# One kernel, two orders of issue: another table of ranks for the same instructions

## The chip, the core and the metric

The kernel runs on one core of one Trainium2 chip. A core has five engines, each with its own stream of instructions that it issues in order: TensorE (PE in the profile, with its weight load PEld), VectorE (DVE), ScalarE (ACT), GpSimd (POOL) and SyncE (SP), which here issues all transfers. The metric is the time of one execution on the device in microseconds, as the median of several runs.

## The reference

`x` is 2048 tokens by 576 channels. The output is the sum of three things: `x`, a spectral filter of the normalised `x`, and a mixture of very small experts on the normalised `x`.

```python
x = A_x
xn = _layernorm(x, axis=-1)
return x + _A_ref(xn, ...) + _B_ref(xn, ...)

# _A_ref: filter in the frequency domain
X = rfft2(x, axes=(-2, -1))
y = irfft2(X * (w_r + 1j * w_i), (S, D))

# _B_ref: 32 heads, two key tables of 8, one expert of 64 for each head and token
q = einsum("nd,dhc->nhc", xf, w_q);  q1, q2 = q[..., :128], q[..., 128:]
i1 = argmax(q1 @ k1.T);  i2 = argmax(q2 @ k2.T)     # K = 1
e = i1 * 8 + i2                                     # the softmax over one candidate is 1
out = sum over heads of gelu(xf . u[e]) * v[e]
```

## The kernel before

**Spectral half.** The two-dimensional transform is split into steps that are matrix products with constant tables. `ln(t, n)` and `folds(t)` normalise a tile of 128 rows and add and subtract its mirrored halves. `dft128(t)`, for 16 tiles, is the first step along the tokens; its results are kept as f16 high and low parts in `AB` and `ABL`. Then come 16 groups `g`. `d_fwd(g)` transforms along the channels, `s_fwd(g)` does the second step along the tokens for two groups at once (it is called for even `g` and makes one pair), `s_mul(g)` multiplies with the spectral weights, `s_inv(g)` and `d_inv(t)` go back. In `s_mul(g)` VectorE makes two products per group (`t1`, `t2`; four per pair), reading PSUM; POOL combines them to `y`; ACT rounds to f16 (`yh`); POOL computes the low part; ACT copies a slice of it to `yl`. `s_inv(g)` needs `yh` and `yl`, and it writes `AB` and `ABL` again by way of ACT and VectorE. The weights of a pair, `Wt`, have three buffers (`Wt_0_110`, `Wt_1_111`, `Wt_2_112`), the tables `s16` four; `load_w(g)` and `load_s16(g)` issue their transfers on SP.

**Expert half.** The keys are folded into the query weights: `fold_part(b, s)` multiplies slices `w` of `w_q` (32 transfers of 576 KB into five buffers) with `KP`, `turned` and `parted` transpose and scale the result into `MU` and `MUL`, 128 rows of heads and keys. `x_t(t)` makes transposed f16 high and low parts of the normalised tile (ACT, POOL `hl`, a transposing transfer on SP). Per block `r` of two tiles, `scores(r)` is one product of `MU` and these, `route(r)` finds the maximum and its index on VectorE (`mx`, `w`, `MT`), and `combine(r)` builds the coefficients of the 64 experts, transposed by TensorE. `fin(t, y)` adds the last step of the inverse transform, the experts' output and `x`, and sends the tile out.

**Order.** The code of these functions doesn't run as it is written. Each call is recorded as an operation of a plan, with its dependencies. Every PSUM tile has one of seven kinds, and at most `LIMIT` tiles of a kind are in flight:

```python
LIMIT = {"x": 2, "a": 4, "b": 4, "c": 4, "s": 2, "f": 1, "m": 2}
```

`a` is `d_fwd` and `d_inv`, `b` is `s_fwd`, `c` is `s_inv`; a tile takes one or two of the eight banks. `forward` then builds the streams: whenever an engine of its model is free, it takes, of the operations whose inputs are there, the one with the smallest number in the table `RANK` (one number for each of 1272 operations). The streams are then issued in that order (line 526, so every instruction has this line in the profile):

```python
_, order, slot, start = self.forward([-r for r in RANK])
...
for i in order:
    for fn, args, kw in ops[i].calls:
        fn(*[x.place() if isinstance(x, _Ps) else x for x in args], ...
```

The same call gives each PSUM tile its place among the banks. On the chip an engine then works through its stream in order and waits at each instruction for what that instruction needs.

Of the kernel before, what the change touches and what calls it, by code (L numbers as in the profile page):

```python
# [32 lines left out]
def _consts():  # L33
# [102 lines left out]
CHANGE = 97.0  # L136

RANK = (
# [63 lines left out]
)  # L202
LIMIT = {"x": 2, "a": 4, "b": 4, "c": 4, "s": 2, "f": 1, "m": 2}
# [1014 lines left out]
```

## Time and profile before

| | us |
|---|---|
| median of 3 runs | 223.99 (223.98 to 224.19) |
| the profiled execution | 224.18 |
| its span in the trace | 222.4 |
| busy: PE | 197.0 (89%) |
| busy: DVE | 190.0 (85%) |
| busy: POOL | 139.8 (63%) |
| busy: ACT | 133.9 (60%) |
| transfers | 48.15 MB, 38.33 read from HBM and 4.72 written there |

The span is what the trace shows from the first to the last event; 1.8 us of the profiled execution lie outside it. Rows of the trace name the tile that is written, an arrow, and the tiles read, with buffer numbers left out: `banks<-s,yh` is a matmul of `s_inv`, `t<-banks,wx,Wt` a product of `s_mul`, `banks<-A,s` is `s_fwd`, `banks<-c,AB` and `banks<-c,ABL` are `d_fwd` or `d_inv`, `banks<-w,KP` is the fold, `banks<-MU,xT` is `scores`. "[0.62 <-DVE t L526]" behind a row says that the engine was idle for 0.62 us ahead of it, and which work ended last that it had waited for.

### The profile page before, as it was taken

How to read it: one execution, taken by the hardware profiler on the slowest of the kernel's cores; microseconds unless marked ns; L12 is line 12 of the kernel's file. 1: busy time of each engine (PE TensorE's matmuls, PEld its weight loads, DVE VectorE, ACT ScalarE, POOL GpSimd, SP SyncE). 2: the span in 40 equal slices, each digit the busy share in tenths (PEclk: the TensorE clock that was granted, in tenths of full speed). 3: DMA queues.
4: the chain of work that ended last, by engine and by line, in shares of the span. 5: the costliest groups of instructions: out<-in, count | busy, mean ns of one | idle time of the engine just before them, and what ended most of it. 6: DMA issues, size and time to landing. Idle time of an engine off the chain costs nothing.

```text
span 222.4 us, 5915 instructions
## 1 busy us (share of the span) xinstructions
PE 197.0 (89%) x2274; PEld 133.6 (60%) x2274; DVE 190.0 (85%) x411; ACT 133.9 (60%) x281; POOL 139.8 (63%) x198
## 2 busy tenths in 40 slices
PE   0289598999998998889999699999999999999993
PEld 0246446785766666675745564654576565678872
DVE  1999999997579978675899989999999998997553
ACT  2279869799938887996686795646541231233320
POOL 2978986860358543794445868769566274657890
PEclk9999979999999999999999999999999999999999
DMA  7999999999999999766170621403452350278935
GB/s 169 378 426 422 406 409 403 392 338 331 302 313 406 288 316 302 193 138 180 42 197 16 160 58 35 111 0 72 92 130 87 106 162 0 60 217 263 409 119 212
DMA packets 33388, 48.15 MB, mean 217 GB/s; under 512 B 20688, under 2 KB 23504, under 8 KB 32976
## 3 DMA queue, kind: packets, MB, share of 16 engines
q1 hardware_dynamic: 33360, 47.77, 66.4%
q8 instruction: 18, 0.29, 0.5%
q14 instruction: 10, 0.08, 0.1%
HBM read 38.33 MB, written 4.72 MB: 194 GB/s over the span
## 4 chain that ended last, share of the span: by engine, by line
PE 56%; DVE 22%; DMA 8%; ACT 5%; issue 4%; POOL 2%; SPq 1%; POOLq 0%; DVEq 0%
PE banks L526 56%; DMA w<-in_wq_dram 7%; DVE t L526 6%; DVE w L526 5%; DVE MT L526 4%; DVE A L526 2%; DMA XN<-in_x_dram 2%; DVE mx L526 1%; DVE AB L526 1%; POOL yh L526 1%; ACT AB L526 1%; DVE sc L526 1%; DVE ABL L526 1%; ACT t L526 1%; ACT yl L526 1%
## 5 line engine op out<-in xcount | busy, mean ns | idle before, releaser
L526 PE MATMUL banks<-MU,xT 128*128 128x512 f16 x192 | 46.8, 379 | 0.7 <-DVE t L526 0.4
L526 POOL TENSOR_TENSOR hl<-XN,hl 128x576 f16<-128x576 f32 x16 | 21.2, 1325 | 24.8 <-ACT hl L526 24.4
L526 PE MATMUL banks<-c,AB 128*128 128x145 f16 (+1 forms) x384 | 35.3, 227 | 0.0
L526 PEld LDWEIGHTS <-xT 128*128 128x128 f16 x224 | 19.7, 98 | 24.1 <-issue 5.5
L526 PEld LDWEIGHTS <-AB 128*128 128x128 f16 x384 | 32.4, 122 | 2.8 <-issue 1.3
L526 POOL TENSOR_TENSOR t<-XN 128x289 f32<-128x289 f32 x32 | 25.3, 809 | 9.3 <-DMA XN<-in_x_dram 3.8
L526 POOL TENSOR_TENSOR A<-t 128x145 f32<-128x145 f32 (+2 forms) x48 | 28.6, 612 | 2.2 <-DVE t L526 0.7
L526 POOL TENSOR_TENSOR y<-t,t 128x289 f32<-128x289 f32 x32 | 22.3, 714 | 10.9 <-DVE t L526 10.5
L526 ACT ACTIVATE yh<-banks,sc 128x580 f32<-128x580 f32 x16 | 11.8, 744 | 24.3 <-PE banks L526 19.3
L526 DVE SCALAR_TENSOR_TENSOR t<-banks,wx,Wt 128x578 f32<-128x578 f32 x32 | 24.5, 808 | 2.0 <-PE banks L526 1.3
L526 POOL TENSOR_TENSOR yh<-y,yh 128x578 f16<-128x578 f32 x16 | 20.7, 1302 | 7.5 <-ACT yh L526 4.2
L526 DVE TENSOR_TENSOR AB<-banks,AB 128x512 f16<-128x512 f32 x32 | 21.7, 680 | 3.9 <-ACT ABL L526 3.3
L526 PE MATMUL banks<-w,KP 128*32 128x288 f32 x256 | 22.4, 449 | 2.5 <-DMA w<-in_wq_dram 1.5
L526 ACT ACTIVATE AB<-banks 128x512 f16<-128x512 f32 x32 | 19.0, 595 | 8.7 <-PE banks L526 8.7
L526 PE MATMUL banks<-Rs,yl 128*99 128x128 f32 x64 | 12.0, 317 | 12.5 <-ACT Rs L526 10.6
L526 PE MATMUL banks<-A,c 128*128 128x288 f32 x64 | 21.7, 421 | 0.5 <-ACT MT L526 0.5
L526 PE MATMUL banks<-c,ABL 99*128 99x289 f16 (+1 forms) x64 | 18.6, 291 | 1.3 <-DVE t L526 0.6
L526 PEld LDWEIGHTS banks<-Rs,yl 128*99 128x99 f32 x64 | 8.7, 186 | 16.8 <-ACT Rs L526 12.6
L526 PEld LDWEIGHTS banks<-Rs,A 128*128 128x128 f32 x128 | 16.4, 203 | 3.2 <-DVE A L526 1.4
L526 DVE TENSOR_REDUCE MT<-w 128x128 bf16<-128x896 bf16 (+1 forms) x16 | 18.2, 1142 | 0.1
L526 PE MATMUL banks<-Rs,A 128*128 128x128 f32 x128 | 18.0, 290 | 0.0
L526 POOL TENSOR_TENSOR t<-yh 128x288 f32<-128x288 f32 x16 | 11.2, 702 | 10.7 <-ACT yh L526 10.6
(106 smaller groups left out, 418.6 us busy)
## 6 DMA issues: line engine op xcount, KB each, us to landing
w<-in_wq_dram SPq DMA_DIRECT2D x32, 576.0 KB, 7.3
Wt<-in_W_dram SPq DMA_DIRECT2D x8, 578.0 KB, 4.3
w<-in_x_dram SPq DMA_DIRECT2D x8, 576.0 KB, 4.6
out_dram<-w SPq DMA_DIRECT2D x14, 288.0 KB, 3.8
XN<-in_x_dram SPq DMA_DIRECT2D x3, 1282.0 KB, 13.4
s<-in_s_dram SPq DMA_DIRECT2D x16, 192.0 KB, 3.1
XN<-in_x_dram SPq DMA_DIRECT2D x2, 641.0 KB, 5.3
c<-in_c_dram SPq DMA_DIRECT2D x1, 868.5 KB, 8.3
```

The costliest lines, as they stand in the source:

```text
L526: fn(*[x.place() if isinstance(x, _Ps) else x for x in args], **{k: x.place() if isinstance(x, _Ps) else x for k, x in kw.items()})
```

## The change

The table `RANK` holds other numbers. Nothing else differs: the same operations with the same dependencies, on the same engines, with the same buffers. By the order in which they come the PSUM tiles get places in the same way as before.

```diff
 RANK = (
-    2, 11, 10, 12, 49, 94, 8, 9, 5, 6, 3, 4, 1, 34, 38, 35, 39, 7, 0, 15, 17, 20, 13, 18, 21, 24, 23, 26, 28,
...
+    33, 36, 55, 25, 37, 40, 56, 57, 45, 63, 14, 16, 19, 28, 22, 42, 31, 98, 66, 107, 111, 97, 101, 44, 39, 50,
...
```

What moves is seen in the streams. Three places follow.

On TensorE, the second pair of spectral groups, before: the end of `s_inv(3)` (tiles `s16_3`, `yl_1`), then two pieces of the fold (`w`, `KP`), the transposes of the folded weights (`c32`, `MT`) and a third piece of the fold, all ahead of `s_inv(2)` (`s16_2`, `yh_0`).

```order
L526 MATMUL banks_66<-s16_3_116,yl_1_104 99x128
L526 MATMUL banks_66<-w_0_117,KP_73 32x288 x4
L526 MATMUL banks_66<-w_3_120,KP_73 32x288 x4
L526 MATMUL banks_66<-c32_68,MT_79 128x128 x3
L526 MATMUL banks_66<-c32_68,wm_81 1x128
L526 MATMUL banks_66<-w_2_119,KP_73 32x288 x4
L526 MATMUL banks_66<-c32_68,MT_79 128x128 x3
L526 MATMUL banks_66<-c32_68,mxr_83 128x1
L526 MATMUL banks_66<-c32_68,MT_79 128x128 x3
L526 LDWEIGHTS yh_0_132
L526 MATMUL banks_66<-s16_2_115,yh_0_132 128x128
```

And after, at the start of `s_inv(2)`, with the end of `d_fwd(7)` (`AB`) ahead of it:

```order
L526 LDWEIGHTS AB_74
L526 MATMUL banks_66<-c16_72,AB_74 128x145
L526 LDWEIGHTS AB_74
L526 MATMUL banks_66<-c16_72,AB_74 128x145
L526 MATMUL banks_66<-w_1_118,KP_73 32x288 x4
L526 MATMUL banks_66<-c32_68,wm_81 1x128
L526 LDWEIGHTS yh_0_132
L526 MATMUL banks_66<-s16_2_115,yh_0_132 128x128
```

`s_inv(2)` has moved ahead of the transposes and of these pieces of the fold, and stands ahead of `s_inv(3)`, behind `d_fwd(6)` and `d_fwd(7)` with one piece of the fold between.

On VectorE, before: the routing of the first block (`mx_0`, `w_2`, `MT`) up to its last sum, then the products of `s_mul(10)` and `s_mul(11)` (`t1`, `t2` with `Wt_0`).

```order
L526 TENSOR_TENSOR w_2_119<-w_2_119,wt_107 128x896
L526 TENSOR_REDUCE MT_79<-w_2_119 128x128
L526 TENSOR_SCALAR wx_82<-banks_66 128x2
L526 RECIPROCAL wx_82<-wx_82 128x2
L526 SCALAR_TENSOR_TENSOR MT_79<-mx_0_127,MT_79 128x128
L526 TENSOR_TENSOR w_2_119<-MT_79,iv_108 128x512
L526 SCALAR_TENSOR_TENSOR MT_79<-MT_79 128x64
L526 TENSOR_TENSOR w_2_119<-w_2_119,MT_79 128x512 x2
L526 TENSOR_REDUCE MT_79<-w_2_119 128x32
L526 SCALAR_TENSOR_TENSOR t1_1_96<-banks_66,wx_82,Wt_0_110 128x578
L526 SCALAR_TENSOR_TENSOR t2_0_105<-banks_66,wx_82,Wt_0_110 128x578
L526 SCALAR_TENSOR_TENSOR t1_0_95<-banks_66,wx_82,Wt_0_110 128x578
```

And after:

```order
L526 SCALAR_TENSOR_TENSOR t1_0_95<-banks_66,wx_82,Wt_0_110 128x578
L526 SCALAR_TENSOR_TENSOR t2_0_105<-banks_66,wx_82,Wt_0_110 128x578
L526 SCALAR_TENSOR_TENSOR t2_1_106<-banks_66,wx_82,Wt_0_110 128x578
L526 TENSOR_TENSOR ABL_75<-banks_66,ABL_75 33x2x128
L526 TENSOR_TENSOR AB_74<-banks_66,AB_74 128x4x128
L526 SCALAR_TENSOR_TENSOR t1_1_96<-banks_66,wx_82,Wt_0_110 128x578
L526 TENSOR_TENSOR AB_74<-banks_66,AB_74 128x4x128
L526 TENSOR_TENSOR ABL_75<-banks_66,ABL_75 33x2x128
L526 TENSOR_REDUCE mx_0_127<-banks_66 128x128
L526 TENSOR_REDUCE mxr_83<-banks_66 1x1
L526 TENSOR_TENSOR w_2_119<-banks_66,mx_0_127 128x896
L526 TENSOR_TENSOR A2_2_99<-banks_66,A2_2_99 128x578
```

The four products of this pair now stand ahead of the first block's maximum `mx_0`, and the routing begins behind them.

On SP, before: the transfers around the weights for `s_mul(4)` and on (`Wt`), with the slices of `w_q` (`w`), the tables `s16` and a transposing transfer between them.

```order
L526 DMA w_2_119<-in_wq_dram 128x1152
L526 DMA Wt_0_110<-in_W_dram 128x1156
L526 DMA w_1_118<-in_wq_dram 128x1152
L526 DMA w_0_117<-in_wq_dram 128x1152
L526 DMA w_3_120<-in_wq_dram 128x1152
L526 DMA s16_1_114<-in_s16_dram 128x768
L526 DMA_TRANSPOSE xT_1_88<-hl_0_122 128x9x128
L526 DMA Wt_1_111<-in_W_dram 128x1156
L526 DMA s16_0_113<-in_s16_dram 128x768
L526 DMA Wt_2_112<-in_W_dram 128x1156
L526 DMA s16_3_116<-in_s16_dram 128x768
L526 DMA w_4_121<-in_wq_dram 128x1152
```

And after, where the same weights are asked for:

```order
L526 DMA w_1_118<-in_wq_dram 128x1152
L526 DMA s16_2_115<-in_s16_dram 128x768
L526 DMA w_0_117<-in_wq_dram 128x1152
L526 DMA Wt_2_112<-in_W_dram 128x1156
L526 DMA s16_3_116<-in_s16_dram 128x768
L526 DMA w_2_119<-in_wq_dram 128x1152
L526 DMA w_3_120<-in_wq_dram 128x1152
L526 DMA Wt_0_110<-in_W_dram 128x1156
L526 DMA w_4_121<-in_wq_dram 128x1152
L526 DMA w_0_117<-in_wq_dram 128x1152
L526 DMA w_1_118<-in_wq_dram 128x1152
```

Here `Wt_2` and the second load of `Wt_0` (the weights of pairs 8 and 10) stand ahead of the last slices of `w_q`; before, `Wt_0` for pair 10 came behind all of them.

Other moves: ahead of the first `d_fwd` the last three tiles of `dft128` change places, and two pieces of the fold (`fold_part(2,0)`) go from just ahead of `d_fwd(0)` to ten operations behind it. The fold as a whole and the transposes to `MU` end later on TensorE; `scores(0)` starts ten operations later; the inverse steps `s_inv` end earlier. At the end the last four output groups are the same, and the transposes of `combine(7)` stand five output groups ahead of the end, where eleven us of work followed them before.

122 rows, old and new, of the table RANK are left out of this document.

## The prediction

> **What bounds the kernel now.** I read the busy time by stretches of the span first, since it shows stage by stage which engine is full. The columns are the stretch, its length, the busy time of TensorE (PE), of the weight load, of VectorE (DVE), ScalarE (ACT) and GpSimd (POOL), then TensorE's granted clock, the DMA share and the rate.
>
> ```profile
> core 0: us, PE busy (x) PEld busy (x) DVE busy (x) ACT busy (x) POOL busy (x), PEclk, DMA share, GB/s
> 0.00:10.00 10.00, 0.28 (x1) 0.29 (x2) 5.19 (x21) 2.64 (x5) 5.47 (x17) 1.00 0.84 259
> 10.00:30.00 20.00, 16.39 (x120) 10.85 (x119) 19.39 (x58) 16.17 (x47) 17.17 (x32) 0.93 1.01 416
> 30.00:50.00 20.00, 18.54 (x171) 14.24 (x164) 18.72 (x45) 16.30 (x45) 14.52 (x23) 0.98 1.01 383
> 50.00:60.00 10.00, 10.00 (x127) 6.87 (x129) 6.52 (x16) 9.95 (x18) 1.28 (x1) 1.00 0.96 311
> 60.00:80.00 20.00, 18.96 (x347) 13.06 (x347) 17.45 (x38) 14.06 (x29) 12.85 (x14) 1.00 1.06 332
> 80.00:100.00 20.00, 17.45 (x319) 13.10 (x318) 15.64 (x37) 17.87 (x35) 12.82 (x15) 1.00 0.85 232
> 100.00:120.00 20.00, 19.59 (x277) 12.01 (x276) 15.95 (x29) 14.88 (x25) 9.85 (x12) 1.00 0.47 121
> 120.00:140.00 20.00, 17.85 (x245) 10.71 (x239) 19.27 (x37) 14.14 (x28) 14.84 (x16) 1.00 0.28 71
> 140.00:200.00 60.00, 58.88 (x546) 37.59 (x545) 58.98 (x118) 22.69 (x47) 36.54 (x53) 1.00 0.37 96
> 200.00:222.40 22.40, 19.01 (x154) 14.93 (x152) 12.88 (x23) 5.21 (x9) 14.47 (x22) 0.99 0.70 250
> sum 222.40, PE 196.97 PEld 133.63 DVE 190.00 ACT 133.91 POOL 139.81; mean PE 19.70 PEld 13.36 DVE 19.00 ACT 13.39 POOL 13.98
> ```
>
> TensorE works 196.97 us and is idle for 25.4. Taken row by row, the idle time is 9.7 us before the first matmul, 5.1 in 10 to 50 (where VectorE is the full engine, 38.1 of 40), 3.6 in 50 to 100, 2.6 in 100 to 140, 1.1 in 140 to 200 and 3.4 in the last row. A change of order can only win from 5.1 + 3.6 + 2.6 + 1.1 = 12.4 us; the rest is the start and the end. From 120 on VectorE is full too (78.25 of 80 us up to 200), so there a wait that is taken from TensorE returns unless VectorE also got ahead.
>
> Then the waits of TensorE, in total and one by one (start, duration, what was idle before and what released it):
>
> ```profile
> PE banks L526 <- DVE t L526: 3.4, 7, 1.0
> ```
>
> ```profile
> 71.09 0.85 PE L526 MATMUL banks<-s,yh 64*128 64x128 f16 x24 [0.62 <-DVE t L526]
> ...
> 85.28 0.30 PE L526 MATMUL banks<-c,ABL 99*128 99x289 f16 x1 [0.40 <-DVE ABL L526]
> ...
> 89.80 0.27 PE L526 MATMUL banks<-c,wm 128*1 128x128 f32 x1 [0.78 <-ACT t L526]
> ...
> 96.67 0.85 PE L526 MATMUL banks<-s,yh 64*128 64x128 f16 x24 [0.54 <-DVE t L526]
> ...
> 123.27 0.85 PE L526 MATMUL banks<-s,yh 64*128 64x128 f16 x24 [1.01 <-DVE t L526]
> ...
> 125.92 0.28 PE L526 MATMUL banks<-c,ABL 99*128 99x289 f16 x1 [0.34 <-DVE t L526]
> ```
>
> The largest single releaser after the start is `DVE t`, the multiplication with the spectral weights in `s_mul`, which frees the PSUM banks of `s_fwd`. `s_inv` cannot be written into them earlier.
>
> **The change, term by term.** No instruction is added or removed, so TensorE's 196.97 us stay. What counts is how much of the 12.4 us of idle time the new order fills.
>
> *Broken runs.* Equal matmuls in a row are cheaper than apart:
>
> ```profile
> 58.20 0.69 PE L526 MATMUL banks<-w,KP 128*32 128x288 f32 x8
> ...
> 63.46 1.18 PE L526 MATMUL banks<-w,KP 128*32 128x288 f32 x16
> ```
>
> Two such groups apart cost 2 × 0.69 − 1.18 = 0.20 us more by busy time; by the starts of the instructions behind them (58.20 to 58.82, 63.46 to 64.57) it is 2 × 0.62 − 1.11 = 0.13. The order has 23 runs of the fold where there were 24, and 158 runs of like groups in all where there were 172. I take −0.1, with ends −0.4 (a few of the other joins worth the same) and 0.
>
> *The start, to 55 us.* TensorE has the same work ahead of the first `d_fwd` (40.3 us by the durations of before). The last three tiles of the first transform change places, and 1.1 us of the fold, the row above of 16 calls, goes from ahead of `d_fwd(0)` to ten places behind it; the loads of weights swap places on SP's queue with the transfers at a share of 1.0. VectorE is the bound, with 1.9 us idle of 40. It cannot gain more than that. I take +0.2, since the fold that leaves was a cover for TensorE while VectorE finished the last tile, and ends −0.5 and +1.1 (the whole fold left uncovered).
>
> *50 to 100 us, waits of 3.6 now.* Pair (2,3) becomes tighter: between the end of `s_fwd(2)` and the first `s_inv` of that pair TensorE has 6.4 us of other work (7.0 before), 7.7 us to the second (12.4 before), by summed durations of the instructions that the order puts there. What the operands need is in these rows, of PE, DVE, POOL and ACT:
>
> ```profile
> 66.73 2.00 PE L526 MATMUL banks<-A,s 64*64 64x289 f16 x48
> ...
> 69.50 2.27 DVE L526 SCALAR_TENSOR_TENSOR t<-banks,wx,Wt 128x578 f32<-128x578 f32 x3
> ...
> 74.22 0.80 DVE L526 SCALAR_TENSOR_TENSOR t<-banks,wx,Wt 128x578 f32<-128x578 f32 x1
> ...
> 66.84 2.53 POOL L526 TENSOR_TENSOR yh<-y,yh 128x578 f16<-128x578 f32 x2
> 69.32 1.21 POOL L526 TENSOR_TENSOR hl<-XN,hl 128x576 f16<-128x576 f32 x1
> 71.19 1.34 POOL L526 TENSOR_TENSOR y<-t,t 128x289 f32<-128x289 f32 x2 [0.66 <-DVE t L526]
> ...
> 75.42 0.52 ACT L526 ACTIVATE yl<-yh 128x396 f16<-128x396 f16 x1
> ...
> 80.81 0.52 ACT L526 ACTIVATE yl<-yh 128x396 f16<-128x396 f16 x1
> ```
>
> `s_fwd(2)` ended at 68.73, the operands were complete at 75.94 and 81.33: 7.2 and 12.6 us later. The second was late because one of its four multiplications stood back on VectorE until 74.22. The new order puts all four together (4 × 0.76 = 3.0 us by the row of three). Then POOL has its y at 3.0 + 1.34 = 4.4, its hl at 5.6, the two low parts at 6.9 and 8.2, and ACT adds 0.52 each: ready at 7.4 and 8.7, against 6.4 and 7.7 of cover. That is a wait of 1.0 in all in place of 0.62. On the other side `d_fwd(8)` now has `s_inv(3)` and two folds more between itself and `s_inv(2)`, whose copies it waited 0.40 for, and pair (4,5) has 8.9 and 12.0 us of cover (7.0 and 9.8 before), so the 0.54 at 96.67 goes. The 0.78 for ACT I halve: ACT is at 17.87 of 20 there, and its work isn't less. Against these stands a new wait. `MU`, the folded weights, is complete only just ahead of its first use:
>
> ```profile
> 95.86 0.27 PE L526 MATMUL banks<-c,xT 128*128 128x128 f32 x1
> ...
> 99.93 0.31 DVE L526 SCALAR_TENSOR_TENSOR MUL<-banks,sc,MUL 128x112 f16<-128x112 f32 x1
> ```
>
> From that last transpose to the last row of `MUL` it took 4.1 us; the new order leaves 1.4 us of TensorE's work between. VectorE does it behind the four multiplications of `s_mul(8)` and `s_mul(9)`. The ends are 2.7 us (as before) and 0 (transpose, copy and scaling at once); I take 0.7, as the copies themselves are short and TensorE is by then not ahead of VectorE by much. Sum: 1.0 + 0.4 + 0.7 and 0.7 for small waits as now = 2.8, so −0.8. The ends are −2.5 (only the 1.0 stays) and +4 (the rival below).
>
> *100 to 140 us, waits of 2.6 now.* `s_inv(9)` waited 1.01 at 123.27 for rows that VectorE had not reached, since the whole of `route(0)` stood ahead of them:
>
> ```profile
> 112.34 1.09 DVE L526 TENSOR_REDUCE mx<-banks 128x128 f32<-128x896 f32 x1 [0.18 <-PE banks L526]
> ...
> 119.82 1.22 DVE L526 TENSOR_REDUCE MT<-w 128x32 f32<-128x1024 bf16 x1
> 120.95 2.26 DVE L526 SCALAR_TENSOR_TENSOR t<-banks,wx,Wt 128x578 f32<-128x578 f32 x3
> ```
>
> That is 8.6 us of routing ahead of `s_mul(10)`; now it stands behind `s_mul(10)` and `s_mul(11)`. Work ahead of `s_mul(10)` on VectorE falls from 101 to 92 us, and on `s_mul(12)` from 114 to 102. The 1.01 and the 0.34 go. What is queued behind is the routing: `scores(0)`'s maximum stands behind 5 us more of VectorE's work, `scores(0)`'s matmuls behind 5.9 us more of TensorE's, so the banks of `scores` come free about when they did against the work around them. I take −1.0; ends −2.0 (0.6 left) and +1.5 (the two largest waits again, for banks of `scores` now).
>
> *After 140 us.* Waits of 1.1 on TensorE, VectorE full. The spectral inverses are done earlier, the routing of the first blocks later, and the sums are equal: 0, ends −0.8 and +1.0.
>
> *The end.*
>
> ```profile
> 207.39 0.28 PE L526 MATMUL banks<-id,MT 128*128 128x128 f16 x2
> ...
> 218.60 0.41 PE L526 MATMUL banks<-vS,MT 128*128 128x288 f16 x2
> ...
> 219.05 0.52 DVE L526 SCALAR_TENSOR_TENSOR w<-banks,sc,w 128x288 f32<-128x288 f32 x1 [0.21 <-PE banks L526]
> ```
>
> The last four output groups are the same. The transposes of `combine(7)` move to 3.7 us ahead of TensorE's end (five groups of 0.73, against 11 us before); VectorE's work ahead of `combine(7)` is unchanged, and its transposes ran at 207.39; 3.7 us ahead of the end is about 214, so they find their input there. 0.
>
> *SP's queue.* The weight loads of `s_mul(4)` to `s_mul(10)` now stand ahead of the last slices for the fold, and SP waits in order for the buffer of each. By the same walk the last three slices are issued when `s_mul(5)` is done, about 84 us, and used from 91 on; with the DMA share at 0.85 in that row they fit. 0.
>
> Sum: −0.1 + 0.2 − 0.8 − 1.0 = −1.7 against the profiled execution's 224.18 us, that is 222.5; the median of the runs, 223.99, lies 0.2 below it. Forecast 222.3.
>
> **Rivals.** *Slower: the pairs need as long as they did.* If POOL and ACT get to the low parts of pair (2,3) no sooner than in before, TensorE waits 0.8 for the first and then 12.6 − 7.7 − 0.8 = 4.1 us for the second, 4.9 in place of the 1.0 that I took: the 2.8 becomes 6.7, and the sum +2.2, that is 226.2. For it speaks ACT at 9.95 of 10 in 50 to 60. Against it speaks that VectorE held back one multiplication, and the new order doesn't. It decides if the second operand comes later than 10.4 us after `s_fwd(2)`, where the added wait eats the 1.7.
>
> *No change: the waits only move.* VectorE is full from 120 on; if TensorE arrives 1.7 us earlier and finds the banks of the routing taken, the time returns by 200. 224.0. Against it: VectorE has 4.4 + 4.1 us idle in 80 to 120 to get ahead in.
>
> *The shared port.* One row of routing shows VectorE held up by POOL:
>
> ```profile
> 114.03 1.28 POOL L526 TENSOR_TENSOR yh<-y,yh 128x578 f16<-128x578 f32 x1 [1.10 <-issue]
> ...
> 114.67 1.12 DVE L526 TENSOR_TENSOR w<-w,wt 128x896 bf16<-128x896 bf16 x1
> ...
> L526 DVE TENSOR_TENSOR w<-w,wt x8: 610/612/1123, 114.7 to 190.2; 128x896 bf16<-128x896 bf16 x8
> ```
>
> It took 1.12 us where the median of eight is 0.61, having begun while POOL's yh ran (to 115.31). The move puts POOL's y and yh of `s_mul(10)` and `s_mul(11)` beside `route(0)`, that is beside four more such operations. At 0.51 us for each, three hits give 1.5 us on a full engine, and the time is 223.8. The other seven of these eight lay clear of it, so I take none.
> The Trainium skill (SBUF — State Buffer, who interferes with whom) says that a VectorE operation with both inputs in SBUF and a GpSimd operation lock each other out for a whole instruction. The rows above agree; by the rule alone all four could be held, and the sum would be 2.0 us worse.
>
> *A larger gain.* If the 0.7 for `MU` and the small waits don't come and VectorE stays ahead, the terms go to −3.3: 220.7.
>
> **Chances.** Near the forecast (221.2 to 223.4) 0.48, larger gain 0.13, waits only moved 0.10 and the port 0.05 (both about 224), slower 0.24. A difference of 0.2% (0.45 us) is about what a measurement tells from none. Faster by more 0.62, within 0.14, slower by more 0.24. The range reaches from the larger gain to the slower case, 220.6 to 225.9; the likeliest case's own is 221.2 to 223.4.
>
> **What would show it.** In the trace after: the wait of `s_inv` on `DVE t` near 123 gone; a wait of about 1 us ahead of pair (2,3) between 68 and 76; the first `MU,xT` matmul at 104 to 105 after a wait below 1 us; TensorE idle below 2 us in 100 to 140; VectorE full from 110 on. I am wrong if the wait ahead of pair (2,3) or of `MU` is over 3 us, or if TensorE's idle time in 140 to 200 grows by what was won before.

## The result, and the profile after

| | before | after |
|---|---|---|
| median, us | 224.04 (223.98 to 224.19, 4 runs) | 226.31 (226.10 to 226.58, 4 runs) |
| ratio | | 1.0101, interval 1.0084 to 1.0119 |
| profiled execution, its span | 224.18, 222.4 | 226.58, 224.7 |

The new order is 1.0% slower, where 0.8% faster was forecast. The page's first lines say what changed at all: VectorE and POOL are each busy for 2 us more, with the same instructions; TensorE works as long as before.

```profile
PE 196.9 (88%) x2274; PEld 133.3 (59%) x2274; DVE 191.9 (85%) x411; ACT 132.6 (59%) x281; POOL 141.8 (63%) x198
```

By stretches of the span, with the columns of before:

```profile
10.00:30.00 20.00, 16.57 (x128) 11.30 (x127) 18.26 (x62) 16.49 (x50) 16.37 (x30) 1.00 1.02 417
30.00:50.00 20.00, 17.30 (x157) 13.18 (x149) 18.29 (x41) 15.68 (x42) 15.30 (x24) 1.00 0.97 366
50.00:60.00 10.00, 9.55 (x137) 7.35 (x141) 6.26 (x15) 7.89 (x16) 1.62 (x2) 1.00 0.77 279
60.00:80.00 20.00, 17.62 (x364) 12.77 (x357) 18.14 (x39) 18.01 (x34) 14.02 (x15) 1.00 0.90 281
80.00:100.00 20.00, 19.34 (x354) 13.29 (x343) 15.94 (x35) 15.77 (x31) 10.45 (x12) 1.00 1.11 313
100.00:120.00 20.00, 18.65 (x276) 12.56 (x272) 14.90 (x31) 17.01 (x32) 12.84 (x14) 1.00 0.53 120
120.00:140.00 20.00, 18.97 (x270) 11.43 (x268) 19.26 (x41) 12.39 (x24) 13.63 (x14) 1.00 0.29 70
140.00:200.00 60.00, 57.32 (x462) 34.66 (x460) 59.28 (x108) 21.57 (x46) 35.90 (x48) 1.00 0.37 104
200.00:224.70 24.70, 21.25 (x165) 16.46 (x162) 16.45 (x29) 5.17 (x8) 16.17 (x24) 1.00 0.60 207
```

From 140 to 200 TensorE is idle for 2.7 us where it was 1.1. Rows of the same time are not the same place in two orders, so I also compared at equal work: the start of the instruction that has so many us of TensorE's work ahead of it, less that work (all by the durations of before). The difference is the idle time up to there.

```
TensorE's work done, us       10    40    60    90   110   120   140   150   170   180   end
idle up to there, before     10.8  14.8  15.8  18.4  20.2  20.5  20.5  20.5  20.9  21.6  21.6
idle up to there, after      10.8  15.3  17.6  19.9  20.0  20.1  20.5  21.9  23.0  23.5  23.9
```

Up to 90 us of work the new order loses 1.5 us, from there to 120 it gets 1.9 back, and at 140 us of work the two are level. Then it loses 2.3 us, as much as the whole difference of the medians. The waits of TensorE in that part are on VectorE:

```profile
159.61 2.75 PE L526 MATMUL banks<-MU,xT 128*128 128x512 f16 x12 [0.34 <-DVE t L526]
170.75 0.75 PE L526 MATMUL banks<-A,c 128*128 128x288 f32 x2 [1.08 <-DVE w L526]
185.36 0.28 PE L526 MATMUL banks<-c,ABL 99*128 99x290 f16 x1 [0.89 <-DVE w L526]
199.30 0.72 PE L526 MATMUL banks<-A,c 128*128 128x288 f32 x2 [0.21 <-DVE w L526]
```

Why VectorE is late is seen in its own rows just ahead of and behind the wait at 170.75, with POOL's rows of the same time below them:

```profile
163.99 1.08 DVE L526 TENSOR_TENSOR w<-banks,mx 128x896 bf16<-128x896 f32 x1
164.99 1.46 DVE L526 TENSOR_SCALAR MT<-MT 128x16 int32<-128x16 f32 x2
166.36 0.61 DVE L526 TENSOR_TENSOR w<-w,wt 128x896 bf16<-128x896 bf16 x1
...
172.75 0.91 DVE L526 TENSOR_TENSOR w<-MT,iv 128x512 bf16<-128x512 bf16 x1
173.58 0.71 DVE L526 SCALAR_TENSOR_TENSOR MT<-MT 128x64 bf16<-128x64 bf16 x1
174.21 0.79 DVE L526 SCALAR_TENSOR_TENSOR MT<-MT,sc,act 128x128 f32<-128x128 int32 x1
...
175.60 1.07 DVE L526 TENSOR_REDUCE MT<-w 128x128 bf16<-128x896 bf16 x1
```

```profile
162.84 1.99 POOL L526 TENSOR_TENSOR A<-t 128x287 f32<-128x287 f32 x3
164.79 1.21 POOL L526 TENSOR_TENSOR hl<-XN,hl 128x576 f16<-128x576 f32 x1
165.95 0.46 POOL L526 TENSOR_TENSOR act<-act,mk 128x128 f32<-128x128 f32 x1
...
170.35 1.35 POOL L526 TENSOR_TENSOR t<-yh 128x288 f32<-128x288 f32 x2 [0.24 <-ACT yh L526]
171.65 3.21 POOL L526 TENSOR_TENSOR A<-t 128x289 f32<-128x289 f32 x4
175.49 0.47 POOL L526 TENSOR_TENSOR MT<-MT 128x128 f16<-128x128 f32 x1 [0.63 <-ACT MT L526]
```

Two scalings of 16 elements take 1.46 us together, and they end when POOL's rows of 164.79 and 165.95 end (166.00 and 166.41). The four `A<-t` of POOL, those of `d_inv`, take 3.21 us, 0.80 each where the mean of before is 0.69 to 0.70. The two engines hold each other up. Not every row is held: `w<-banks,mx`, which reads one of its inputs from PSUM, has its usual 1.08 us at 163.99 beside POOL's `A<-t` and `hl`, and the reduction at 175.60 its usual 1.07 beside POOL's `MT<-MT`. To have one number for it, I call stretch what a VectorE row that overlaps a POOL row takes beyond the shortest duration of the same kind of row in any of the runs here (rows of 0.1 us and more over; such a sum is good to some 0.3 us). After 140 us the stretch is 2.8 us in before and 7.9 in after, in 8 rows there and in 18 here. Before had such rows too; these two are the largest, of a kind that takes 0.27 us when it is free:

```profile
184.80 0.78 DVE L526 SCALAR_TENSOR_TENSOR MT<-mx,MT 128x128 bf16<-128x128 f32 x1
...
194.53 0.79 DVE L526 SCALAR_TENSOR_TENSOR MT<-mx,MT 128x128 bf16<-128x128 f32 x1
```

### The profile page after: what moved, and what is told of

Same layout as the page of the kernel before. It is cut to its first block, busy times and chain, and to the rows that moved or that the text cites. A ratio compares the mean times of both kernels' runs of the same rounds, so it can differ in the third digit from the quotient of the medians.

```text
span 224.7 us, 5923 instructions
## 1 busy us (share of the span) xinstructions
PE 196.9 (88%) x2274; PEld 133.3 (59%) x2274; DVE 191.9 (85%) x411; ACT 132.6 (59%) x281; POOL 141.8 (63%) x198
## 4 chain that ended last, share of the span: by engine, by line
PE 43%; DVE 36%; DMA 7%; issue 5%; ACT 4%; POOL 3%; DVEq 0%; POOLq 0%
PE banks L526 43%; DVE w L526 9%; DVE MT L526 9%; DVE t L526 6%; DMA w<-in_wq_dram 5%; DVE A L526 3%; DVE AB L526 3%; POOL t L526 2%; DMA XN<-in_x_dram 2%; DVE mx L526 2%; DVE ABL L526 1%; DVE sc L526 1%; ACT AB L526 1%; ACT ABL L526 1%; DVE st L526 1%
## 5 line engine op out<-in xcount | busy, mean ns | idle before, releaser
L526 POOL TENSOR_TENSOR A<-t 128x145 f32<-128x145 f32 (+2 forms) x48 | 30.6, 654 | 4.7 <-DVE t L526 3.0
L526 POOL TENSOR_TENSOR hl<-XN,hl 128x576 f16<-128x576 f32 x16 | 19.9, 1244 | 19.3 <-ACT hl L526 19.3
L526 POOL TENSOR_TENSOR y<-t,t 128x289 f32<-128x289 f32 x32 | 21.8, 701 | 14.5 <-DVE t L526 14.0
L526 POOL TENSOR_TENSOR t<-XN 128x289 f32<-128x289 f32 x32 | 24.0, 768 | 9.8 <-DVE A L526 4.2
L526 PE MATMUL banks<-w,KP 128*32 128x288 f32 x256 | 21.7, 433 | 2.4 <-DVE AB L526 1.8
L526 PE MATMUL banks<-Rs,yl 128*99 128x128 f32 x64 | 11.2, 305 | 13.5 <-ACT Rs L526 10.0
L526 POOL TENSOR_TENSOR yh<-y,yh 128x578 f16<-128x578 f32 x16 | 21.9, 1388 | 1.7 <-ACT yh L526 0.8
L526 PE MATMUL banks<-Rs,A 128*128 128x128 f32 x128 | 18.5, 293 | 0.0
```

## The experiments

Ratios are to runs of the kernel before on the same chip, with their 95% intervals; the new table has 1.0101 (1.0084 to 1.0119). "Old" and "new" are the two tables.

| run | ratio | stretch after 140 us | TensorE's idle time from 140 us of work to the end |
|---|---|---|---|
| old (before) | 1 | 2.8 | 1.1 |
| new (after) | 1.0101 | 7.9 | 3.4 |
| e3, new, POOL's late work off | 0.9889 (0.9860 to 0.9917) | 0.4 | −0.4 |
| e4, old, the same | 1.0040 (1.0011 to 1.0069) | 0.3 | 1.0 |
| e7, new, only d_inv off POOL | 0.9892 (0.9862 to 0.9922) | 1.6 | −0.4 |
| e14, old, the same | 0.9991 (0.9971 to 1.0012) | 0.3 | 0.7 |
| e6, new, only x_t's late low parts off | 0.9994 (0.9979 to 1.0010) | 5.7 | 2.1 |
| e5, new, as e3, and POOL reads again | 1.0126 (1.0094 to 1.0159) | 9.1 | 4.7 |
| e9, new, POOL's work in halves | 1.0114 (1.0062 to 1.0166) | 6.8 | 3.1 |
| e11, new, only d_inv in halves | 1.0093 (1.0061 to 1.0126) | 6.9 | 3.7 |
| e10, old, POOL's work in halves | 1.0052 (1.0025 to 1.0079) | 5.0 | 3.4 |
| e12, new, scalings by ScalarE | 0.9967 (0.9953 to 0.9980) | 5.5 | 1.0 |
| e13, old, scalings by ScalarE | 1.0124 (1.0093 to 1.0154) | | |
| e1, new to 140 us, then old | 1.0264 (1.0221 to 1.0308) | | |
| e2, old to 140 us, then new | 1.0204 (1.0170 to 1.0238) | | |
| e8, new, routing ahead of s_mul(10) | 1.0376 (1.0329 to 1.0423) | | |

(A negative idle time means that TensorE's instructions were a little shorter there than in before. The last four have another order of TensorE, in which the columns don't compare. In e3 to e7 and e14 ScalarE copies one input where POOL made a sum or a difference; these kernels leave the sums out and give other outputs, so they serve as tests of the time only.)

**Where in the program: two spliced orders.** The ranks were numbered anew: one table's order up to the 860th operation, then the rest in the order of the other.

> Ranks: the new table's order up to its 860th operation (about 139 us), then the old table's order for all that is left. Theory L (the loss of 2.3 us arises after 140 us, where VectorE is full and its routing instructions are stretched by POOL's in the new order): 223.6 to 224.8, as at 140 us both orders stand within 0.3 us of each other. Rival H (the loss is laid by the changed head and spectral part, which leaves less work or fuller buffers behind): 225.8 to 226.8.

> Ranks: the old table's order up to its 860th operation (about 140 us), then the new table's order for all that is left. Theory L: 225.5 to 226.6, the loss comes with the late order alone. Rival H: 223.6 to 224.6.

Both are 2% and more slower than the old table and 1.6% and 1.0% slower than the new one, so they decide nothing. At the seam the state of one order meets the sequence of the other: in e1 TensorE waits 0.89 and 3.50 us for VectorE's `ABL` behind it, in e2 0.96 and 1.03 for `yh` and `yl`. An order can't be judged by halves.

**POOL's late work taken away.** The plan and its order stay, row by row. Where POOL made a sum or a difference of two tiles, ScalarE now copies one of them: the engine changes, and the arithmetic is left out.

```diff
+    def copy_late(o, i, j):
+        plan.add("gpsimd", lambda x, y, z: nc.scalar.activation(x, y, AF.Copy), "tensor_tensor", (o, i, j), {})
...
-        G.tensor_tensor(y[:, 0:289], eo[:, 0, :], eo[:, 1, :], op=OP.add)
+        copy_late(y[:, 0:289], eo[:, 0, :], eo[:, 1, :])
```

> The new table, each engine's order unchanged, but POOL's late operations (those of d_inv, the low parts in combine, and the low parts of x_t from tile 12 on) are done as plain copies by ScalarE: the sums and differences are left out, the sizes and the places stay. Theory P (the shared SBUF port: VectorE's instructions with SBUF inputs are held until POOL's end): VectorE's routing rows after 140 us go back to their shortest durations, 3 to 5 us less of VectorE's busy time, and the time falls to 221.5 to 223.5, to within 0.7 us of the same edit of the old table. Rival W (waits by the order of issue itself, whatever POOL does): 225.5 to 226.5, 2 us or more above the same edit of the old table.

> The old table with the same edit. Theory P: VectorE loses 2 to 3.5 us of busy time after 140 us, the time falls to 221.5 to 223.5. Rival W: 223.5 to 224.2, and 2 us or more below the new table with the edit.

The new table goes from 1.0101 to 0.9889, and TensorE has no wait of 0.2 us or more left from 140 us to its end. In the old one TensorE's last matmul stays where it was (starting at 218.51 against 218.60), so there the stretch cost nothing. The runs of e4 are 1 us slower all the same: its span is 1.5 us longer with the work of TensorE and VectorE done at the same time, so the added time lies behind them. In the trace most of it is the last output transfer, which is issued at 219.50 and lands at 222.52, 3.0 us later; in before it took 1.8 (219.60 to 221.37). Why it is late is open. Five of ten executions took 224.45 to 224.73 us and the others 225.6 and more, so it may be late in some of them only. A cleaner pair was needed: only the three operations of each `d_inv`.

> The new table, only the three POOL operations of each d_inv as copies by ScalarE (sums and differences are left out). Theory P: the stretches after 170 us go (about 5 us of VectorE rows, of which TensorE waited for 2 to 3): 223.0 to 224.6. Rival Q: if it is the delivery to fin, the same gain but with VectorE's routing rows unchanged in length.

> The old table with only the POOL operations of d_inv as copies by ScalarE (sums and differences left out), the counterpart of e7. Theory O (the new order is the better one without the port, by the 1 to 2 us that were forecast): 223.3 to 224.2, above e7's 222.2 by 1.1 to 2.0. Rival: the old order gains as much as the new one lost, 222.0 to 222.6, and the order itself is worth nothing.

Here are the rows of VectorE in e7 that answer to those above:

```profile
163.53 1.07 DVE L523 TENSOR_TENSOR w<-banks,mx 128x896 bf16<-128x896 f32 x1
164.53 0.23 DVE L523 TENSOR_SCALAR MT<-MT 128x16 int32<-128x16 f32 x2
164.68 0.61 DVE L523 TENSOR_TENSOR w<-w,wt 128x896 bf16<-128x896 bf16 x1
...
171.04 0.42 DVE L523 TENSOR_TENSOR w<-MT,iv 128x512 bf16<-128x512 bf16 x1
171.37 0.22 DVE L523 SCALAR_TENSOR_TENSOR MT<-MT 128x64 bf16<-128x64 bf16 x1
171.51 0.34 DVE L523 SCALAR_TENSOR_TENSOR MT<-MT,sc,act 128x128 f32<-128x128 int32 x1
```

The 1.46 is 0.23, the 0.91 is 0.42, the 0.71 is 0.22 and the 0.79 is 0.34, while `w<-banks,mx`, which reads PSUM, is as it was (1.08 and 1.07). POOL is idle beside all of these rows of e7. Without POOL's share of `d_inv` the new order is at 0.9892 and the old at 0.9991: the new order is then the better one by 1.0%, clear of both intervals. That this is about what was forecast for it (0.8%) is in part luck: by the last column 1.1 us of the gain arise behind 140 us of work, where the forecast had nothing, and not between 50 and 140, where it had 1.8. The 2.1% (4.7 us) by which the new table itself is slower than e7 go with POOL's three operations of `d_inv`.

That e3 gains no more than e7 says that `d_inv` is the part that counts; the low parts of `x_t` alone bring half of it:

```diff
+            if t < 12:
+                G.tensor_tensor(w[:, 640:], XN[:, t, :576], w[:, :576], op=OP.subtract)
+            else:
+                copy_late(w[:, 640:], XN[:, t, :576], w[:, :576])
```

> The new table, only the low parts of x_t from tile 12 on as copies by ScalarE (the differences are left out). Theory P: the three VectorE rows that ended with such a POOL row (0.53 at 148.8, 0.61 at 155.1, 1.24 at 165) go, 1.0 to 2.2 us less: 224.2 to 225.3. Rival Q: 226.0 to 226.6, since scores waits long for the transposes anyway.

e6 has 0.9994, 1.1% below the new table, or some 2.4 us, for 2.2 us less stretch; its 224.43 us lie in the range of theory P. The gains of e6 and e7 don't add up to more than e3's, since after either of them TensorE has little left to wait for.

**Reading, or delivering late?** In e3 ScalarE also delivers sooner than POOL did. So POOL got its reading back, with nobody waiting for its result:

```diff
+        def both(x, y, z):
+            nc.scalar.activation(x, y, AF.Copy)
+            s = view(RM[:, 608:1152], x.shape, x.dtype)
+            nc.gpsimd.tensor_tensor(s, y, z, op=OP.subtract)
```

> The new table with ScalarE's copies as in e3, and beside each copy POOL does a difference of the same two inputs, of the same size and at its old place, into memory that nobody reads. Nobody waits for POOL's results, so POOL's lateness is gone and its reading of SBUF is back. Theory P (the port): VectorE's rows are stretched again, 225.3 to 226.8. Rival Q (what helped e3 is that ScalarE delivers sooner than POOL): 221.8 to 223.0, as e3.

All of the loss returns (1.0126). TensorE's waits of 1.08 and 0.89 us in after are there again, and a third stands ahead of a `scores` (`MU,xT`), though of another block:

```profile
169.76 0.75 PE L523 MATMUL banks<-A,c 128*128 128x288 f32 x2 [1.14 <-DVE w L523]
180.46 2.75 PE L523 MATMUL banks<-MU,xT 128*128 128x512 f16 x12 [0.73 <-DVE t L523]
185.31 0.29 PE L523 MATMUL banks<-c,ABL 99*128 99x290 f16 x1 [0.94 <-DVE w L523]
```

So POOL's late delivery is out. There is one more way in which POOL could be late, by keeping a buffer that it still reads; in e5 the others wait for that for 0.8 us behind 140 us (VectorE 0.6, ScalarE 0.2), TensorE not at all, and e3, without these readers, is 2.4% faster. What remains is POOL's work in SBUF beside VectorE. It reads two tiles and writes one, and no run here parts the two.

**Shorter holds.** If VectorE is held to the end of one POOL instruction, instructions of half the length should halve it.

```diff
-        G.tensor_tensor(y[:, 0:289], eo[:, 0, :], eo[:, 1, :], op=OP.add)
+        in_halves(y[:, 0:289], eo[:, 0, :], eo[:, 1, :], op=OP.add)
```

> The new table, nothing left out and no place changed; each of POOL's operations of d_inv and each low part (x_t, s_mul) is issued as two of half the size, so that each holds the SBUF port half as long at a time. Theory P (VectorE is held to the end of one POOL instruction): the stretches after 140 us halve and the waits of TensorE with them, 223.5 to 225.3. Rival (VectorE loses the same share of its time however POOL's work is cut): 226 to 227, or more, from the added instructions.

> The new table with only the operations of d_inv in halves. Theory P: nearly all of the gain of the run with all in halves, since taking d_inv's work off POOL brought all that taking everything off brought: 223.8 to 225.5. Rival: no gain, 226 to 227.

> The old table with the same edit. Theory P with slack: VectorE's late stretches cost nothing here (the old table with no late POOL work had its last matmul at the same time), so only the early ones count, above all the 1.28 and 1.12 us rows at 114 to 118 ahead of s_mul(10): 223.0 to 224.2. Rival: the added POOL instructions make y and yh late for s_inv, 224.4 to 226.

My expectation fell in all three. In e11 a half takes 0.476 us in the mean where the whole took 0.73:

```profile
L551 POOL TENSOR_TENSOR t<-yh 128x144 f32<-128x144 f32 x32 | 14.5, 476 | 5.2 <-ACT yh L523 5.1
```

The stretch falls by 1 us only: the holds are shorter and more. In after 18 rows are held by 0.45 us in the mean; in e11 it is 22 rows by 0.32, in e9 24 by 0.29. POOL also needs longer, and TensorE waits for its `A` near the end (0.65 us in e9, 0.41 in e11), which it didn't in after. In the old order the cut even adds stretch (2.8 to 5.0) and time, and TensorE waits 0.42 and 0.41 us for POOL's `A`, which it didn't before.

**Relief of VectorE with the results kept.** If VectorE's time after 140 us is what the new order lacks, any work taken from it should help.

```diff
-            V.tensor_scalar(ci[:, :, w], cw[:, w]..., 2.0 ** (18 + 30 * w), None, op0=OP.mult)
+            A.activation(ci[:, :, w], cw[:, w]..., AF.Copy, scale=2.0 ** (18 + 30 * w))
```

> The new table; the two scalings to whole numbers in each combine (16 rows of VectorE, 4.1 us busy in the new order, 2.5 in the old) are done by ScalarE, with the same results; VectorE's order shifts by a few rows. Theory V (VectorE's time after 140 us is the bound there, so a relief of 4 us comes back at the 0.6 us per us that the other runs gave): 223.6 to 225.0. Rival R (VectorE now waits for ScalarE between two rows of one block, 0.5 us for each of eight blocks): 226 to 228.

> The old table with the same edit. Theory V: TensorE waited little after 140 us in the old order, so little is to be had: 223.0 to 224.2. Rival R: 224.5 to 226.

e12 is the fastest kernel here that computes everything: 223.80 us against 224.54 on the same chip, 0.9967 (0.9953 to 0.9980) of the kernel before and 1.3% below the new table. One large wait of TensorE is left behind 160 us (1.34 on `DVE w` at 170.23). The same edit makes the old order slower (1.0124), by more than even the rival had it: it ends with two waits, for VectorE (0.26 at this place in before) and for POOL's last `d_inv` (none before),

```profile
198.60 0.28 PE L523 MATMUL banks<-c,ABL 99*128 99x290 f16 x1 [1.18 <-DVE w L523]
220.03 0.75 PE L523 MATMUL banks<-A,c 128*128 128x288 f32 x2 [1.64 <-POOL A L523]
```

The edit also shifts a few rows of the order (20 of TensorE's operations, by up to 4 places, in e13; none in e12), so e13's loss may be one of order; the two were not tried apart.

**The move ahead of the routing, undone.** Operations 855 to 888 are the four products of `s_mul(10)` and `s_mul(11)`, 600 is the first sum of `combine(0)`.

```diff
+        for i in (855, 856, 887, 888):
+            ops[i].deps.add(600)
```

> The new table with one order put back: the products of s_mul(10) and s_mul(11) may come only behind the first sum of combine(0), so that the routing of the first two blocks goes ahead of them on VectorE, as in the old order. Theory S (the later routing took VectorE's slack, so that each stretch after 150 us becomes a wait of TensorE): 224.0 to 225.5, with a new wait of about 1 us for s_inv(10). Rival M (my step in the prediction: the move itself was a gain of 1.0 to 1.4): 227.0 to 228.0.

With the products behind the routing of the first blocks the time rises to 1.0376. It is more than an undoing: TensorE then waits 3.00 us at 140.62 for the weights' scale and 4.09 us at 164.52 for `ABL`, since everything behind these products is late. Neither theory had this; it gives no support to the idea that the later routing as such does harm.

## Why the prediction was wrong

*Broken runs* (−0.1): too small to be seen.

*The start* (+0.2, ends −0.5 to +1.1): +0.5 at 40 us of work, within the ends. In after TensorE waits 1.81 us for VectorE's `AB` at 35.34, where before a wait for a slice of `w_q` of 1.48 stood at 25.69.

*50 to 100 us* (−0.8): the sign was wrong. Between 40 and 90 us of work the new order loses 1.0 us where it was to win 0.8. 0.68 of it is a stall that the profile puts down to issue and that e7, with the same order up to there, doesn't have, so some 0.3 us belong to the order. The waits I had named came small: none ahead of the pair (2,3) for its operands, and 0.28 and 0.20 ahead of the first `MU,xT`, only the second of them for `MU`, where I had put 0.7. I missed others:

```profile
72.43 0.30 PE L526 MATMUL banks<-c,ABL 99*128 99x289 f16 x1 [0.70 <-DVE ABL L526]
...
76.64 0.38 PE L526 MATMUL banks<-c,mxr 128*128 128x1 f32 x2 [0.90 <-DVE mxr L526]
```

The first is `d_fwd(7)`, two groups behind `s_inv(1)`: VectorE's `ABL` that it waited for ended at 72.38 and is the last copy out of the banks of an `s_inv`. The second is a tiny product for the scale of a pair's weights, which now stands between `s_inv(2)` and `s_inv(3)` and holds the rest of TensorE's queue until VectorE has come to its maximum.

*100 to 140 us* (−1.0): right in kind, and larger. From 90 to 120 us of work the idle time grows by 0.2 us in after and by 2.1 in before (to 140, by 0.6 and 2.1); the waits at 123.27 and 125.92 for `DVE t` are gone, and of their kind 0.21 is left at 126.31. By rows of time TensorE is idle for 2.4 us from 100 to 140, not below 2 as I had said, because the stall of 0.68 falls there.

*After 140 us* (0, ends −0.8 to +1.0): this is the step that failed. Of the 4.0 us between the forecast's −1.7 and the +2.3 that came, 2.3 arise here; the other 1.7 are those of the two terms up to 100 us, less the surplus of the one above. "The sums are equal" took VectorE's durations as constants. TensorE's idle time there grew by 2.3 us more than in before, beyond the end that I had set, because VectorE's rows stretched by 7.9 us in place of 2.8. I had the mechanism in hand, with the right price for a hit (0.51 us; the four rows shown above lost 1.23, 0.49, 0.49 and 0.45), and put it in the wrong place: I looked for it beside `route(0)`, where `s_mul(10)` goes, and took none because seven of eight rows of one kind lay clear of it in before. (Beside `route(0)` little changed indeed: of these eight rows one is held in after too, 1.05 us at 122.63.) Those seven only told how the old order's rows fell against POOL's, and one kind of row told nothing of the others: the `MT<-mx,MT` rows of before shown above were held for 0.5 us each. That VectorE was full there (58.98 of 60 us) should have told me that each hit counts. The prediction's own sign came true: TensorE's idle time in 140 to 200 grew, from 1.1 to 2.7 us.

The Trainium skill (SBUF — State Buffer, Who interferes with whom) has the rule: a VectorE instruction with two SBUF inputs and a GpSimd instruction that reads SBUF exclude each other, whichever comes first holding the port for its whole length, and `tensor_scalar` may belong to the same group. The traces agree, to the row (0.91 against 0.42 us, and 1.46 against 0.23 for two `tensor_scalar`). By that rule I gave 2.0 us, at the price of four hits beside `route(0)`; against e7 the hits of the whole stretch cost 2.1% of the time, 4.7 us.

*The end* (0): right. From the end of the last matmul to the end of the span it is 3.4 us in both. *SP's queue* (0): right. TensorE's waits for slices of `w_q` come to 0.2 us in after (1.5 in before).

*The rivals.* "The shared port" had the true mechanism, with a chance of 0.05, the wrong place and a time (223.8) that assumed three hits. "Slower: the pairs need as long as they did" (0.24) had the right time (226.2) by luck: there was no wait ahead of pair (2,3) for its operands. "The waits only move" supposed a TensorE that comes 1.7 us early to the full VectorE; at 140 us of work it was level.

What stays open: why the stretch is 2.8 us in one order and 7.9 in the other. POOL's reading rows and VectorE's routing rows are the same; only how they fall against each other differs (18 rows held in place of 8), and nothing here says which of the moves brought them together.

## What to carry to other kernels

Where two engines hold each other up, as VectorE and POOL do here (0.91 us in place of 0.42), durations belong to the order and not to the instruction alone: when a change moves work on a full engine, list the rows on it that can be held and the rows on the other engine that will run beside them in the new order, over the whole stretch in which the engine is full, not just at the place that is moved. A row that was not held in one order tells nothing of the next. An order is also best judged with the suspected coupling taken out (the same order, with the other engine's reading given to a third engine): here that alone told a good order from a bad meeting of rows.

## What the runs showed of the hardware that I had not expected

- A VectorE operation on 16 elements per partition took 1.05 us in place of 0.15: it ended when a POOL operation on 576 did, which had begun 0.2 us ahead of it.
- The hold goes both ways: POOL's `A<-t` rows of `d_inv` take 0.80 us in the stretch shown, and 0.69 to 0.70 in the mean of before.
- Halving POOL's instructions costs 2 × 0.476 us in place of 0.73 and takes little from the stretch (7.9 to 6.9 us in e11).
- One profiled run of the new order has a stall of 0.68 us of TensorE at 100.77 with no releaser; other runs with the same order there don't.
